# Scores in 64x64 quarters of the array, block sums of the values in column strips, and the weights' low parts on GpSimd, in an attention + ReLU² feed-forward kernel

## The chip, the cores and the metric

The kernel runs on one core of a Trainium2 chip. The metric is the device time of one execution in microseconds (us), smaller is better. The core has a matrix engine (PE in the profile), a vector engine (DVE), an activation engine (ACT), a general one (POOL, called GpSimd in the code) and a queue that issues the transfers (SP). Three runs of the kernel before gave a median of 666.93 us (666.03 to 668.0).

## The reference

What is computed, cut to its core (4 batches, 8 heads, 768 tokens, head size 64, in 32-bit floats):

```python
k_sum = k.reshape(B, H, nb, 32, D).max(axis=3)        # nb = 24 blocks of 32 keys
v_sum = v.reshape(B, H, nb, 32, D).mean(axis=3)
mask_l = np.abs(pos[:, None] - pos[None, :]) < 16
scores_l = where(mask_l, scale * q @ k.T, -1e9)
scores_s = scale * q @ k_sum.T + np.log(32)
a = softmax(concatenate([scores_l, scores_s]))
x = (a @ concatenate([v, v_sum])).transpose(0, 2, 1, 3).reshape(3072, 512)
h = x @ w_in                                          # 512 -> 2048
out = (np.maximum(h, 0) ** 2) @ w_out                 # 2048 -> 512
```

## The kernel before, in words

**Attention.** The 3072 tokens are cut into 48 groups `g` of 64 queries, twelve to a batch. Each group sees 118 keys: the 24 block maxima, and the 94 keys that its window can reach. The steps of one group, with the names of its tasks:

- `S` (L462): scores. Four matmuls, one for each pair of heads, 128 rows x 118 columns. The host lays the queries of a pair out as a 128x128 block with zeros off the diagonal, so that the two heads of a pair don't mix (`qW`, 256 KB a group).
- `M`, `X` (DVE, L484 and L494), `E` (ACT, L503), `R` (DVE, L512 and L513), `N` (POOL, L519): mask and scale, row maximum, exponentials, reciprocal of the sum, and its product.
- `T`: the weights are transposed so that keys lie on partitions. For `g < NPE` (16) on PE (L532) with a copy by ACT; for the others on DVE in 32x32 squares (L549), which then go out to DRAM (L560) and back (L566) to bring the squares to their places.
- `V` (L578): values. Eight matmuls, one for each head, 118 rows x 64 columns; even heads land in the upper and odd heads in the lower 64 columns of the array.
- `XH` (ACT, L588), `XL` (DVE, L591): the result is split into a high part, rounded to the matrix engine's one-pass 32-bit form, and a low part.

**Feed-forward.** A unit `u` is 8 groups (512 tokens), and there are six; 16 hidden blocks `f` of 128 make up 96 items. An item is 12 matmuls of the input product (`FI`, L676, tile `h`: high x high, low x high, high x low for four slices of 128), ReLU and square, a split again, and 12 matmuls of the output product (`FO`, L702, tile `o`). In the last item of a unit `FO` is cut into four pieces, one for each tile of 128 tokens, and each is copied out (`PC`, L727 and L729).

**Weights and values.** The weights arrive as 64-bit floats and are turned into high and low parts in the first unit (`WM` ACT, `WR` `WJ` `WS` DVE L624 L630 L636, `WH` ACT L641, low part `WW` DVE L644), 32 times. The block means of the values: `batch_v_pe` for batches 0 and 1 (six matmuls 24x512 against a matrix of 1/32, `VM` L355, and one copy); `batch_v` for batches 2 and 3 (sums on DVE, L389, and small transfers, L413, from a second layout of `v`).

**What sets the order.** `Plan` simulates the engines with a cost for each task, a due time and the buffers' slots, and writes the instructions of every engine in that order; at run time each engine works its list off in order, held by semaphores. PSUM (the matrix engine's output memory) holds eight banks: four `o`, two `h`, two `att`. `att` serves in turn the scores, the transposes, the values and the block sums of batch 1; before unit 0 the scores use the four `o` banks.

Of the kernel before, what the change touches and what calls it, by code (L numbers as in the profile page):

```python
# [10 lines left out]
F32 = mybir.dt.float32  # L11
# [9 lines left out]
P = 128  # L21
BLOCK = 32
WINDOW = 16
TQ = 64
# [9 lines left out]
NPE = 16  # L34
# [139 lines left out]
def attention_then_relu2_ffn(  # L174
# [4 lines left out]
    v: bass.AP,  # L179
# [5 lines left out]
    B, H, S, D = v.shape  # L185
# [27 lines left out]
    def o_buf(name, cols=512):  # L213
        return buf("o", 4, (P, cols), F32, name, ps)
# [4 lines left out]
    def att_buf(name, cols=512):  # L219
        return buf("att", 2, (P, cols), F32, name, ps)  # L220
# [10 lines left out]
    T0, SLOW, STEP = 35.0, 7.1, 6.5  # L231
# [55 lines left out]
    for g in reversed(range(NG)):  # L287
        pairs = (P, NPAIR, P)
        if g < EARLY:
            q_bufs[g], v_bufs[g] = lend(f"qv{g}", pairs, None)  # L290
            p_bufs[g], a_bufs[g] = lend(f"pa{g}", pairs, None)
        else:
            q_bufs[g] = buf("q", 2, pairs, F32, f"q{g}")
# [44 lines left out]
    def batch_v_pe(b):  # L338

        key = wanted(b * NW) - 28 if b else -60  # L340
        out_ps = (att_buf if b else o_buf)(f"vps{b}")
        vs = vs_bufs[b] = buf("vs", 1, (NB, DM), F32, f"vs{b}")
        last = None
        for i in range(S // P):
            x = buf("half", 4, (P, DM), F32, f"fv{b}_{i}") if b else first_v[i]
            whole = b > 0 or i % 2 == 0
            t = add(
                f"FV{b}_{i}", "SP", 0.45,
                lambda i=i, x=x: nc.sync.dma_start(out=x.tile, in_=vS[b, i * P : (i + 1) * P, :]),
                key - 4 + i, behind=None if whole else t, take=[x] if whole else [], use=[] if whole else [x],  # L350
                size=4 * P * DM, begin=key - 10 if b else 0,
            )

            def mm(i=i, x=x):
                nc.tensor.matmul(  # L355
                    out_ps.tile[:NB], lhsT=means[:, i * NB : (i + 1) * NB], rhs=x.tile,
                    start=(i == 0), stop=(i == S // P - 1),
                )

            last = add(  # L360
                f"VM{b}_{i}", "PE", 0.87, mm, key + i, [t, t_means, last],
                take=[out_ps] if i == 0 else [], use=[x] + [out_ps] * (i > 0),
            )
        t_VS[b] = [add(
            f"VS{b}", "ACT", 0.55, lambda: nc.scalar.copy(out=vs.tile, in_=out_ps.tile[:NB]), key + 7, [last],
            take=[vs], use=[out_ps],
        )]

    def batch_v(b):
        key = wanted(b * NW) - 28  # L370
        n = 512 // D
        nq = BLOCK // n
        vs = vs_bufs[b] = buf("vs", 1, (NB, DM), F32, f"vs{b}")
        after = []
        for hg in range(H // 4):
            part = buf("part", 1, (4 * NB, nq + 1, D), F32, f"part{b}_{hg}")
            src = v[b, 4 * hg : 4 * hg + 4].rearrange("h (j r) d -> (h j) r d", r=BLOCK)
            sums = []
            for i in range(nq):
                raw = buf("half", 4, (P, DM), F32, f"vr{b}_{hg}_{i}")  # L380

                def view(raw=raw):
                    return raw.tile[: 4 * NB].rearrange("p (r d) -> p r d", d=D)

                def load(i=i, src=src, view=view):
                    nc.sync.dma_start(out=view(), in_=src[:, i * n : (i + 1) * n, :])

                def reduce(i=i, part=part, view=view):
                    nc.vector.tensor_reduce(  # L389
                        out=part.tile[:, i, :], in_=view().rearrange("p r d -> p d r"), op=ALU.add, axis=AX.X  # L390
                    )

                t = add(f"VL{b}_{hg}_{i}", "SP", 0.45, load, key, take=[raw], size=4 * 96 * 512, begin=key - 4)
                sums.append(
                    add(f"VR{b}_{hg}_{i}", "DVE", 1.02, reduce, key + 1, [t],
                        take=[part] if i == 0 else [], use=[raw] + [part] * (i > 0))
                )
                if i:
                    sums[-1].after.append(sums[0])

            def total(part=part):
                x = part.tile
                nc.vector.tensor_reduce(
                    out=x[:, nq, :], in_=x[:, :nq, :].rearrange("p i d -> p d i"), op=ALU.add, axis=AX.X
                )
                nc.vector.tensor_scalar_mul(x[:, nq, :], x[:, nq, :], 1.0 / BLOCK)

            t = add(f"VT{b}_{hg}", "DVE", 0.75, total, key + 2, sums, use=[part])
            for hh in range(4):

                def put(hh=hh, hg=hg, part=part):
                    h = 4 * hg + hh
                    nc.sync.dma_start(out=vs.tile[:, h * D : (h + 1) * D], in_=part.tile[hh * NB : (hh + 1) * NB, nq, :])  # L413

                first = hg == hh == 0
                after.append(
                    add(f"VP{b}_{hg}_{hh}", "SP", 0.45, put, key + 3, [t] + after[:1],
                        take=[vs] if first else [], use=[part] + [vs] * (not first), size=6144)
                )
        t_VS[b] = after  # L420


    def attention(g):
# [7 lines left out]
        lq = add(f"QL{g}", "SP", 0.45, lambda: nc.sync.dma_start(out=q.tile, in_=qW[g]), due - 26, take=[q], size=4 * P * DM, begin=due - 36)  # L431
# [26 lines left out]
        s_ps = (o_buf if g < UG else att_buf)(f"s{g}", NPAIR * KEYS)  # L458

        def scores():  # L460
            for p in range(NPAIR):
                nc.tensor.matmul(  # L462
                    s_ps.tile[:, p * KEYS : (p + 1) * KEYS], lhsT=q.tile[:, p, :], rhs=kb[:, p, k0 : k0 + KEYS],
                    start=True, stop=True,
                )
# [3 lines left out]
        t_S[g] = add(f"S{g}", "PE", 0.95, scores, due - 15, deps, take=[s_ps], use=[q])  # L469
# [11 lines left out]
        def masked():  # L481
            if pr.first:
                nc.gpsimd.memset(pr.tile[:, :, KEYS:], 0.0)  # L483
            nc.vector.scalar_tensor_tensor(  # L484
                out=pr.tile[:, :, :KEYS], in0=s_ps.tile.rearrange("p (n k) -> p n k", k=KEYS),
                scalar=1.0 / math.sqrt(D), in1=masks[off].unsqueeze(1).broadcast_to([P, NPAIR, KEYS]),
                op0=ALU.mult, op1=ALU.add,
            )
# [38 lines left out]
        if wide:  # L527
            at_ps = att_buf(f"t{g}")
# [43 lines left out]
        x_ps = (h_buf if g < UG else att_buf)(f"x{g}", NPAIR * TQ)  # L572
        old = [t_FI[(g - RING) // UG, NF - 1]] if g >= RING else []

        def values():
            av = a.tile.rearrange("k (i n r) -> k i n r", i=NSQ, n=NPAIR)
            for h in range(H):
                nc.tensor.matmul(  # L578
                    x_ps.tile[h % 2 * D : (h % 2 + 1) * D, h // 2 * TQ : (h // 2 + 1) * TQ],
                    lhsT=vv.tile[:KEYS, h * D : (h + 1) * D],  # L580
                    rhs=av[:KEYS, h % 2 * 2 : h % 2 * 2 + 2, h // 2, :], start=True, stop=True,
                )
# [4 lines left out]
        def high():  # L587
            nc.scalar.copy(out=xh[:, :, cols], in_=x_ps.tile.rearrange("p (n t) -> p n t", n=NPAIR))  # L588

        def low():  # L590
            nc.vector.tensor_tensor(  # L591
                out=xl[:, :, cols], in0=x_ps.tile.rearrange("p (n t) -> p n t", n=NPAIR),
# [10 lines left out]
    def convert(f, n):  # L603
# [39 lines left out]
        def low():  # L643
            nc.vector.tensor_tensor(  # L644
# [10 lines left out]
        t7 = add(f"WW{name}", "DVE", 0.7, low, due - 4.5, [t6], use=[w, t])  # L655
# [5 lines left out]
    def ffn(u, f, o, done):  # L661
# [37 lines left out]

        def outer(todo):  # L700
            for t, i in todo:
                nc.tensor.matmul(  # L702
                    o[t].tile, lhsT=terms[i][0].tile[:, t * P : (t + 1) * P], rhs=terms[i][1].tile,
# [9 lines left out]
        for i, piece in enumerate(pieces):  # L713
# [3 lines left out]
                take=[o[i]] if first else [], use=[gh, gl] + ([] if first else [o[i]] if last else o),  # L717
            )
            done.append(t6)
            if last:  # L720
                put(u, i, o[i], t6, due + 0.1 * i)

    def put(u, i, o, t, due):
        rows = slice(u * TU + i * P, u * TU + (i + 1) * P)
        x = buf("half", 4, (P, DM), F32, f"os{u}_{i}")
        if i % 2:
            t2 = add(f"PC{u}_{i}", "ACT", 0.62, lambda: nc.scalar.copy(out=x.tile, in_=o.tile), due + 0.6, [t], take=[x], use=[o])  # L727
        else:
            t2 = add(f"PC{u}_{i}", "DVE", 0.7, lambda: nc.vector.tensor_copy(out=x.tile, in_=o.tile), due + 0.6, [t], take=[x], use=[o])  # L729
# [4 lines left out]
    batch_v_pe(0)  # L734
    done_g = 0

    def groups(n):
        nonlocal done_g
        while done_g < n:
            g = done_g  # L740
            b, w = divmod(g, NW)
            if b and not w:
                batch_k(b)
                (batch_v_pe if b < 2 else batch_v)(b)
# [8 lines left out]
    for u in range(NU):  # L753
        groups((u + 1) * UG)
        o = [o_buf(f"o{u}_{t}") for t in range(NTT)]
# [56 lines left out]
```

## Time and profile before

| what | before |
|---|---|
| median of three runs | 666.93 us (666.03 to 668.0) |
| profiled execution | 667.02 us |
| its span (first to last instruction) | 665.3 us |
| PE busy | 643.5 us, 97% |
| DVE / ACT / POOL busy | 340.3 / 278.6 / 83.6 us |
| mean granted clock of PE | 0.994 |

The span lies 1.7 us under the profiled execution's time; that execution stands within 0.1 us of the median. A matrix product of two full 32-bit operands (scores, values, block sums) is two instructions on PE, and one of the one-pass form (`FI`, `FO`) is one; so `x8` behind a score row is a group's four matmuls.

### The profile page before, as it was taken

Reading aid. Unit: us, or ns where it says so; the run is one execution under the profiler, and the core shown is the slowest. Engines: PE = TensorE matmul, PEld = TensorE weight load, DVE = VectorE, ACT = ScalarE, POOL = GpSimd, SP = SyncE. Lnnn points to the kernel's source line nnn. Section 1 sums busy time; section 2 is a strip of 40 time slices with the busy share of each in tenths; the row PEclk is TensorE's granted clock in tenths of the full one; section 3 lists DMA queues with packets and bytes.
Section 4 is the critical chain, followed back from the end, with each engine's and each line's share of the span. In section 5 each row is a group of like instructions: output and inputs, shape, how many; then the busy total and the mean of one; then the engine's idle time right before and its main releaser. Section 6 shows DMA issues by size and latency. Waiting matters only on the chain.

```text
span 665.3 us, 9719 instructions
## 1 busy us (share of the span) xinstructions
PE 643.5 (97%) x3544; PEld 511.2 (77%) x3544; DVE 340.3 (51%) x612; ACT 278.6 (42%) x751; POOL 83.6 (13%) x140
## 2 busy tenths in 40 slices
PE   4979999999999999999999999899999999999997
PEld 3557668878887878787888877778878888888886
DVE  4698879985433375644434586443553342322222
ACT  2688559775534443433323432233343242222221
POOL 3741001100201001101110200110110010000000
PEclk9979999999999999999999999999999999999999
DMA  9955657502523381633141482322352311000001
GB/s 308 323 196 180 237 213 245 187 24 75 157 76 80 78 256 42 182 88 76 49 115 45 150 254 75 101 73 75 97 149 56 91 34 33 32 33 1 0 1 63
DMA packets 50215, 75.61 MB, mean 114 GB/s; under 512 B 6440, under 2 KB 22824, under 8 KB 50168
## 3 DMA queue, kind: packets, MB, share of 16 engines
q1 hardware_dynamic: 50168, 75.00, 36.8%
q8 instruction: 28, 0.46, 0.3%
q14 instruction: 19, 0.16, 0.1%
HBM read 59.75 MB, written 14.68 MB: 112 GB/s over the span
## 4 chain that ended last, share of the span: by engine, by line
PE 86%; DVE 4%; SPq 4%; DMA 3%; issue 1%; POOL 1%; ACT 0%; DVEq 0%; ACTq 0%; POOLq 0%
PE h L676 38%; PE o L702 37%; PE s L462 6%; PE x L578 4%; PE vps L355 2%; SPq L560 1%; DMA vr<-v 1%; DVE part L389 1%; DMA fv_lent<-vS 1%; PE t L532 1%; SPq L440 1%; SPq L413 1%; POOL qv_lent L443 0%; DMA a<-turn 0%; DMA out<-os 0%
## 5 line engine op out<-in xcount | busy, mean ns | idle before, releaser
L676 PE MATMUL h<-xh,w 128*128 128x512 f32 x768 | 245.7, 401 | 0.5 <-ACT xh L588 0.5
L702 PE MATMUL o<-w,gh 128*128 128x512 f32 x768 | 203.9, 400 | 0.0
L676 PEld LDWEIGHTS h<-xh,w 128*128 128x128 f32 x768 | 143.2, 189 | 35.0 <-issue 0.8
L702 PEld LDWEIGHTS o<-w,gh 128*128 128x128 f32 x768 | 139.8, 188 | 32.3 <-issue 1.7
L676 PE MATMUL h<-xl,w 128*128 128x512 f32 x384 | 152.8, 398 | 0.3 <-DVE xl L591 0.3
L684 ACT ACTIVATE r<-h 128x512 f32<-128x512 f32 x96 | 57.2, 595 | 183.6 <-PE h L676 159.9
L695 DVE TENSOR_TENSOR gl<-r,gh 128x512 fp32r<-128x512 f32 x96 | 69.1, 720 | 85.4 <-PE o L702 53.8
L702 PE MATMUL o<-w,gl 128*128 128x512 f32 x384 | 109.2, 391 | 0.0
L690 DVE TENSOR_TENSOR r<-r 128x512 f32<-128x512 f32 x64 | 44.8, 700 | 96.8 <-ACT r L684 95.7
L692 ACT CAST gh<-r 128x512 fp32r<-128x512 f32 x96 | 59.6, 621 | 77.7 <-PE o L702 48.9
L676 PEld LDWEIGHTS h<-xl,w 128*128 128x128 f32 x384 | 72.7, 189 | 18.5 <-DVE xl L591 1.0
L702 PEld LDWEIGHTS o<-w,gl 128*128 128x128 f32 x384 | 72.1, 188 | 15.8
L503 ACT ACTIVATE p<-p,nm 128x118 f32<-128x118 f32 x160 | 61.1, 384 | 49.0 <-DVE nm L494 49.0
L519 POOL TENSOR_TENSOR p<-p,nm 128x472 f32<-128x472 f32 x40 | 45.1, 1128 | 184.4 <-DVE nm L513 106.9
L474 POOL COPY kb<-kb 128x96 f32<-128x96 f32 x44 | 17.1, 389 | 275.8 <-PE s L462 271.7
L462 PEld LDWEIGHTS s<-kb,q 128*128 128x128 f32 x320 | 41.6, 191 | 5.2 <-POOL p L483 1.2
L462 PE MATMUL s<-kb,q 128*128 128x118 f32 x320 | 42.1, 274 | 1.0 <-POOL p L483 1.0
L484 DVE SCALAR_TENSOR_TENSOR p<-s,mask 128x472 f32<-128x472 f32 x40 | 25.8, 645 | 26.0 <-PE s L462 25.5
L578 PEld LDWEIGHTS x<-a,v 118*64 118x64 f32 x640 | 22.0, 137 | 17.6 <-issue 12.4
L549 DVE STREAM_TRANSPOSE a<-p 128x512 f32<-128x512 f32 x32 | 22.7, 708 | 19.6 <-POOL p L519 19.6
L512 DVE TENSOR_SCALAR nm<-nm 128x4 f32<-128x4 f32 x48 | 8.9, 185 | 44.9 <-ACT p L503 43.5
L578 PE MATMUL x<-a,v 118*64 118x64 f32 x640 | 27.4, 228 | 3.5 <-DMA a<-turn 2.9
(55 smaller groups left out, 423.3 us busy)
## 6 DMA issues: line engine op xcount, KB each, us to landing
raw<-wW SPq DMA_DIRECT2D x32, 512.0 KB
q<-qW SPq DMA_DIRECT2D x40, 256.0 KB
turn<-a SPq DMA_DIRECT2D x128, 64.0 KB
a<-turn SPq DMA_DIRECT2D x32, 256.0 KB
v<-vS SPq DMA_DIRECT2D x36, 192.0 KB
kb<-kT SPq DMA_DIRECT2D x16, 384.0 KB
out<-os SPq DMA_DIRECT2D x24, 256.0 KB
vr<-v SPq DMA_DIRECT2D x16, 192.0 KB
```

Source lines behind the costliest of these rows:

```text
L462: nc.tensor.matmul(s_ps.tile[:, p * KEYS : (p + 1) * KEYS], lhsT=q.tile[:, p, :], rhs=kb[:, p, k0 : k0 + KEYS], start=True, stop=True,)
L484: nc.vector.scalar_tensor_tensor(out=pr.tile[:, :, :KEYS], in0=s_ps.tile.rearrange("p (n k) -> p n k", k=KEYS), scalar=1.0 / math.sqrt(D), ...
L503: nc.scalar.activation(x, x, AF.Exp, bias=nm.tile[:, p : p + 1], scale=1.0, accum_out=nm.tile[:, NPAIR + p : NPAIR + p + 1],)
L519: nc.gpsimd.tensor_tensor(out=x, in0=x, in1=nm.tile[:, 2 * NPAIR :].unsqueeze(2).broadcast_to([P, NPAIR, KEYS]), op=ALU.mult)
L549: nc.vector.transpose(out=a.tile.rearrange("p (j n r) -> p j n r", j=NSQ, n=NPAIR), in_=pr.tile.rearrange("p n (j c) -> p j n c", c=SQ),)
L578: nc.tensor.matmul(x_ps.tile[h % 2 * D : (h % 2 + 1) * D, h // 2 * TQ : (h // 2 + 1) * TQ], lhsT=vv.tile[:KEYS, h * D : (h + 1) * D], rhs= ...
L676: nc.tensor.matmul(h.tile, lhsT=lhs.tile[:, k * P : (k + 1) * P], rhs=rhs[:, k, c0 : c0 + TU], start=(i == 0), stop=(i == 3 * KT - 1),)
L684: t2 = add(f"RL{u}_{f}", "ACT", 0.62, lambda: nc.scalar.activation(r.tile, h.tile, AF.Relu), due + 3, [t1], take=[r], use=[h])
L690: lambda: nc.vector.tensor_tensor(out=r.tile, in0=r.tile, in1=r.tile, op=ALU.mult), due + 4, [t2], use=[r],
L692: t4 = add(f"GH{u}_{f}", "ACT", 0.62, lambda: nc.scalar.copy(out=gh.tile, in_=r.tile), due + 5, [t3], take=[gh], use=[r])
L695: lambda: nc.vector.tensor_tensor(out=gl.tile, in0=r.tile, in1=gh.tile.bitcast(F32), op=ALU.subtract),
L702: nc.tensor.matmul(o[t].tile, lhsT=terms[i][0].tile[:, t * P : (t + 1) * P], rhs=terms[i][1].tile, start=(first and i == 0), stop=(last an ...
```

## The change

Five things change.

1. **Scores.** Each head is a matmul of its own, 64 rows x 64 columns of the array: `score_of(h)` gives the quarter and the place. Heads of a pair `p` read rows 0-63 (even) and 64-127 (odd); the columns alternate, so that the four heads of two pairs name all four quarters. The host stores the queries without the zeros, 128 KB a group.
2. **PSUM.** One tile `att` of two banks is no longer two slots: scores take its columns 0-117 in four slices, the values take columns 192-255 or 128-191 (two slots). The scores thus have one slot. The four `o` tiles become two, each of two banks, and a tile of 128 tokens is a half of one. Transposes and block sums take `h` slots.
3. **Transposes.** `NPE` is 8: groups 8 to 15 are transposed by DVE and sent through DRAM, as those from 16 on were.
4. **Block sums.** All four batches take the matrix engine; each 24x512 matmul is cut into four of 24x128, each in its own strip of 32 columns, and four copies gather them. The sums on DVE and the second layout of `v` are gone.
5. **Low parts of the weights** (`WW`) go from DVE to POOL. The planner's constants change with it (`T0`, `STEP`, the costs of `S`, `VM`, `VS`, `WW`).

```diff
-NPE = 16
+NPE = 8
...
+    att = ps.tile([P, 4, 256], F32, name="att", bufs=1)
+            kinds["s"] = Slots(None, "s", 1, [att])
+            kinds["x"] = Slots(None, "x", 2, [att[:, :, 256 - (i + 1) * TQ : 256 - i * TQ] for i in range(2)])
+    def score_of(h):
+        p, r = divmod(h, 2)
+        return 2 * r + p // 2, r ^ p % 2
...
-                nc.tensor.matmul(
-                    out_ps.tile[:NB], lhsT=means[:, i * NB : (i + 1) * NB], rhs=x.tile,
-                    start=(i == 0), stop=(i == S // P - 1),
-                )
+                for c in range(NSQ):
+                    nc.tensor.matmul(
+                        out_ps.tile[c * SQ : c * SQ + NB, :P], lhsT=means[:, i * NB : (i + 1) * NB],
+                        rhs=x.tile[:, c * P : (c + 1) * P], start=(i == 0), stop=(i == S // P - 1),
+                    )
...
-            for p in range(NPAIR):
+            for h in range(H):
+                p, r = divmod(h, 2)
+                j, c = score_of(h)
+                rows = slice(r * D, (r + 1) * D)
                 nc.tensor.matmul(
-                    s_ps.tile[:, p * KEYS : (p + 1) * KEYS], lhsT=q.tile[:, p, :], rhs=kb[:, p, k0 : k0 + KEYS],
-                    start=True, stop=True,
+                    s_ps.tile[c * TQ : (c + 1) * TQ, j, :KEYS],
+                    lhsT=q.tile[rows, p, :], rhs=kb[rows, p, k0 : k0 + KEYS], start=True, stop=True,
                 )
...
-            nc.vector.tensor_tensor(
+            nc.gpsimd.tensor_tensor(
                 out=w.tile[:, DM:], in0=t.tile, in1=w.tile[:, :DM].bitcast(F32), op=ALU.subtract
             )
...
+        def o_of(o, t):
+            return o[t // 2].tile.rearrange("p (a b) c -> p a (b c)", a=2)[:, t % 2]
...
-                take=[o[i]] if first else [], use=[gh, gl] + ([] if first else [o[i]] if last else o),
+                take=[o[i // 2]] if first and i % 2 == 0 else [],
+                use=[gh, gl] + ([o[i // 2]] * (i % 2) if first else [o[i // 2]] if last else o),
```

Where instructions move is seen on PE at three places.

First, the start of the program on PE before: scores (`s`), block sums of batch 0 (`vps`), transposes (`t`) and values (`x`).

```order
L462 MATMUL s_167<-kb,qv_lent 128x118 x4
L462 MATMUL s_180<-kb,qv_lent 128x118 x4
L355 MATMUL vps_190<-fv_lent,means 24x512
L462 MATMUL s_203<-kb,qv_lent 128x118 x4
L355 MATMUL vps_190<-fv_lent,means 24x512 x2
L532 MATMUL t_230<-ident,pa_lent 128x128 x4
L355 MATMUL vps_190<-fv_lent,means 24x512
L462 MATMUL s_241<-kb,qv_lent 128x118 x4
L355 MATMUL vps_190<-fv_lent,means 24x512
L532 MATMUL t_254<-ident,pa_lent 128x128 x4
```

And the same place on PE after the change, up to the first values (`att`).

```order
L434 MATMUL s_166<-kb,qv_lent 64x118 x8
L375 MATMUL vps_182<-fv_lent,means 24x128 x4
L434 MATMUL s_189<-kb,qv_lent 64x118 x8
L375 MATMUL vps_182<-fv_lent,means 24x128 x8
L434 MATMUL s_220<-kb,qv_lent 64x118 x8
L375 MATMUL vps_182<-fv_lent,means 24x128 x12
L434 MATMUL s_262<-kb,qv_lent 64x118 x8
L504 MATMUL t_279<-ident,pa_lent 128x128 x4
L504 MATMUL t_294<-ident,pa_lent 128x128 x4
L434 MATMUL s_304<-kb,qv_lent 64x118 x8
L551 MATMUL att<-pa_lent,qv_lent 64x64 x8
```

Three scores stand ahead of the first transpose before and four after, all block sums of batch 0 are done ahead of the first transpose, and the numbers of matmuls double for scores and go fourfold for block sums. On DVE, the list ahead of the last low part (`XL`) of unit 0's values holds four `WJ`, three `WS`, two `WW` and nine `M` before, and two `WJ`, two `WS`, no `WW` and ten `M` after; its other work there is the same.

Second, the end of unit 1 on PE, where batch 2 begins. Before, the scores of a group (`s`) stand between the input product of the unit's last item (`h`) and an output product (`o`); no block sums stand there.

```order
L676 MATMUL h_15_2451<-xl,w_15_1565 128x512
L462 MATMUL s_2468<-kb,q_2271 128x118 x4
L702 MATMUL o_0_1805<-w_13_1547,gh_13_2389 128x512 x2
L702 MATMUL o_1_1838<-w_13_1547,gh_13_2389 128x512 x2
L702 MATMUL o_2_1850<-w_13_1547,gh_13_2389 128x512 x2
L702 MATMUL o_3_1867<-w_13_1547,gh_13_2389 128x512 x2
L702 MATMUL o_0_1805<-w_13_1547,gl_13_2414 128x512
```

After the change the six pieces of batch 2's block sums (`vps`) lie between the products of the unit's last items.

```order
L375 MATMUL vps_2493<-fv_1_2463,means 24x128 x4
L678 MATMUL o_0_1902<-w_12_1546,gh_12_2425 128x512 x4
L678 MATMUL o_1_1947<-w_12_1546,gh_12_2425 128x512 x4
L678 MATMUL o_0_1902<-w_12_1546,gl_12_2437 128x512 x2
L678 MATMUL o_1_1947<-w_12_1546,gl_12_2437 128x512 x2
L375 MATMUL vps_2493<-fv_2_2465,means 24x128 x4
L551 MATMUL att<-a_2427,v_74 64x64 x8
L375 MATMUL vps_2493<-fv_3_2468,means 24x128 x4
L434 MATMUL att<-kb,q_2482 64x118 x8
L375 MATMUL vps_2493<-fv_4_2511,means 24x128 x4
```

Each of these pieces waits for one load of 128 tokens of `v`; scores, values and block sums now stand side by side between two products.

Third, the last output products on PE, with the semaphores that they wait for. Before, the four tiles `o_0` to `o_3` follow each other, and only the first waits for its operands.

```order
L702 MATMUL o_0_5181<-w_15_1610,gl_15_5567 128x512 [waits DVE_49]
L702 MATMUL o_1_5199<-w_15_1610,gh_15_5565 128x512 x2
L702 MATMUL o_1_5199<-w_15_1610,gl_15_5567 128x512
L702 MATMUL o_2_5203<-w_15_1610,gh_15_5565 128x512 x2
L702 MATMUL o_2_5203<-w_15_1610,gl_15_5567 128x512
L702 MATMUL o_3_5207<-w_15_1610,gh_15_5565 128x512 x2
L702 MATMUL o_3_5207<-w_15_1610,gl_15_5567 128x512
```

After, each of the two tiles holds two outputs, and the second output of a tile waits for the copy of the first.

```order
L678 MATMUL o_0_5332<-w_15_1703,gl_15_5716 128x512 [waits DVE_49]
L678 MATMUL o_0_5332<-w_15_1703,gh_15_5714 128x512 [waits DVE_49]
L678 MATMUL o_0_5332<-w_15_1703,gh_15_5714 128x512
L678 MATMUL o_0_5332<-w_15_1703,gl_15_5716 128x512
L678 MATMUL o_1_5353<-w_15_1703,gh_15_5714 128x512 x2
L678 MATMUL o_1_5353<-w_15_1703,gl_15_5716 128x512
L678 MATMUL o_1_5353<-w_15_1703,gh_15_5714 128x512 [waits DVE_49]
L678 MATMUL o_1_5353<-w_15_1703,gh_15_5714 128x512
```

The two waits for DVE in the rows `o_0 ... gh` and `o_1 ... gh` are new; they are for the copies of the first and the third output (L705 of the new kernel).

More of the change, by code (lines that the diff above doesn't have):

```diff
@@ L360, in batch_v_pe @@
             last = add(
-                f"VM{b}_{i}", "PE", 0.87, mm, key + i, [t, t_means, last],
+                f"VM{b}_{i}", "PE", 0.3, mm, key + i, [t, t_means, last],
                 take=[out_ps] if i == 0 else [], use=[x] + [out_ps] * (i > 0),
             )
[L364 to L420, printed above, removed]
@@ L423, in attention, with gather @@
+        def gather():
+            for c in range(NSQ):
+                nc.scalar.copy(out=vs.tile[:, c * P : (c + 1) * P], in_=out_ps.tile[c * SQ : c * SQ + NB, :P])
+        t_VS[b] = [add(f"VS{b}", "ACT", 1.1, gather, key + 7, [last], take=[vs], use=[out_ps])]
     def attention(g):
@@ L429, in attention @@
         wide = NPE > g
-        lq = add(f"QL{g}", "SP", 0.45, lambda: nc.sync.dma_start(out=q.tile, in_=qW[g]), due - 26, take=[q], size=4 * P * DM, begin=due - 36)
+        lq = add(f"QL{g}", "SP", 0.45, lambda: nc.sync.dma_start(out=q.tile, in_=qW[g]), due - 26, take=[q], size=2 * P * DM, begin=due - 36)
         def load_v():
@@ L484, in masked @@
             nc.vector.scalar_tensor_tensor(
[L485 removed]
+                out=pr.tile[:, :, :KEYS], in0=s_ps.tile[:, :, :KEYS],
                 scalar=1.0 / math.sqrt(D), in1=masks[off].unsqueeze(1).broadcast_to([P, NPAIR, KEYS]),
@@ L587, in high @@
         def high():
-            nc.scalar.copy(out=xh[:, :, cols], in_=x_ps.tile.rearrange("p (n t) -> p n t", n=NPAIR))
+            nc.scalar.copy(out=xh[:, :, cols], in_=x_ps.tile)
         def low():
             nc.vector.tensor_tensor(
-                out=xl[:, :, cols], in0=x_ps.tile.rearrange("p (n t) -> p n t", n=NPAIR),
+                out=xl[:, :, cols], in0=x_ps.tile,
                 in1=xh[:, :, cols].bitcast(F32), op=ALU.subtract,
@@ L654, in convert @@
         t6 = add(f"WH{name}", "ACT", 0.62, high, due - 5.5, [t5], take=[w], use=[t])
-        t7 = add(f"WW{name}", "DVE", 0.7, low, due - 4.5, [t6], use=[w, t])
+        t7 = add(f"WW{name}", "POOL", 1.25, low, due - 4.5, [t6], use=[w, t])
         t_W[n, f] = [t6, t7]
@@ L726, in put @@
         if i % 2:
-            t2 = add(f"PC{u}_{i}", "ACT", 0.62, lambda: nc.scalar.copy(out=x.tile, in_=o.tile), due + 0.6, [t], take=[x], use=[o])
+            t2 = add(f"PC{u}_{i}", "ACT", 0.62, lambda: nc.scalar.copy(out=x.tile, in_=o_tile()), due + 0.6, [t], take=[x], use=[o])
         else:
-            t2 = add(f"PC{u}_{i}", "DVE", 0.7, lambda: nc.vector.tensor_copy(out=x.tile, in_=o.tile), due + 0.6, [t], take=[x], use=[o])
+            t2 = add(f"PC{u}_{i}", "DVE", 0.7, lambda: nc.vector.tensor_copy(out=x.tile, in_=o_tile()), due + 0.6, [t], take=[x], use=[o])
         add(f"PS{u}_{i}", "SP", 0.45, lambda: nc.sync.dma_start(out=out[rows, :], in_=x.tile), due + 1, [t2], use=[x], size=4 * P * DM)
     batch_k(0)
-    batch_v_pe(0)
+    batch_v(0)
     done_g = 0
@@ L754, in attention_then_relu2_ffn @@
         groups((u + 1) * UG)
-        o = [o_buf(f"o{u}_{t}") for t in range(NTT)]
+        o = [o_buf(f"o{u}_{t}") for t in range(NTT // 2)]
         for f in range(NF):
```

53 lines of the change are left out of this document (28 added, 25 removed).

## The prediction, as made before the changed kernel was run

> **What bounds the kernel now.** I read the page first, for the busy shares and the chain that ended last.
>
> ```profile
> span 665.3 us, 9719 instructions
> PE 643.5 (97%) x3544; PEld 511.2 (77%) x3544; DVE 340.3 (51%) x612; ACT 278.6 (42%) x751; POOL 83.6 (13%) x140
> PE 86%; DVE 4%; SPq 4%; DMA 3%; issue 1%; POOL 1%; ACT 0%; DVEq 0%; ACTq 0%; POOLq 0%
> PE h L676 38%; PE o L702 37%; PE s L462 6%; PE x L578 4%; PE vps L355 2%; SPq L560 1%; DMA vr<-v 1%; DVE part L389 1%; DMA fv_lent<-vS 1%; PE t L532 1%; SPq L440 1%; SPq L413 1%; POOL qv_lent L443 0%; DMA a<-turn 0%; DMA out<-os 0%
> ```
>
> PE is the bound: it carries 86% of the chain, and three quarters of the chain are feed-forward products, which the change leaves alone. What is to be had lies in scores (6%), values, block sums and transposes, and where PE waits. The windows by stage show where it waits (columns: window, us, then busy us and instructions of PE, PEld, DVE, ACT, POOL, the granted clock, DMA share, GB/s).
>
> ```profile
> 10.00:20.00 10.00, 9.43 (x31) 4.55 (x30) 4.85 (x13) 5.12 (x25) 2.91 (x8) 1.00 1.05 339
> 20.00:30.00 10.00, 8.48 (x78) 6.01 (x78) 6.33 (x15) 7.41 (x31) 6.27 (x14) 1.00 1.05 317
> 30.00:40.00 10.00, 7.74 (x106) 6.59 (x104) 9.74 (x20) 8.04 (x27) 8.37 (x15) 1.00 0.63 222
> 100.00:120.00 20.00, 20.00 (x126) 16.45 (x125) 18.36 (x36) 18.03 (x46) 3.22 (x4) 1.00 0.74 250
> 400.00:500.00 100.00, 97.09 (x553) 78.53 (x552) 48.31 (x87) 34.37 (x104) 12.54 (x16) 1.00 0.35 96
> ```
>
> From 100 us on PE is full; before, DVE is (9.74 of 10 us from 30 to 40). So there are two regimes: in the steady part every piece on PE costs its own length; at the start the end is set by when the first input product can begin.
>
> **Scores.** The chain of waits from 215 us gives pieces as start, length and what; each length runs to the next start.
>
> ```profile
> 218.07 2.80 PE h L676 x12
> 220.87 0.88 PE s L462 x8
> 221.75 2.76 PE o L702 x12
> 224.51 0.61 PE x L578 x16
> 225.13 3.00 PE h L676 x12
> 228.13 2.76 PE o L702 x12
> ```
>
> A group's scores cost 0.88 us: eight instructions of 118 columns, 0.11 each, one after another. The values show what half-width pieces do: 16 instructions take 0.61, and the product behind them 3.00 instead of 2.80, so 0.81 in all. If one 64-column pass takes 0.11 x 64/118 = 0.06, sixteen in a row would take 0.96; two halves side by side take 0.48. A timeline cut at three ends shows how they start (the columns are start, length, what, and the count inside the window).
>
> ```profile
> 314.97 0.28 PE L578 MATMUL x<-a,v 118*64 118x64 f32 x2
> 314.97 0.39 PE L578 MATMUL x<-a,v 118*64 118x64 f32 x6
> 311.24 0.26 PE L462 MATMUL s<-kb,q 128*128 128x118 f32 x1
> ```
>
> The first window ends at 315.00, the second at 315.14: two have started after 0.03 us, six after 0.17, so a pair starts every 0.06. The third is the same cut for the scores of before: 0.08 us in, one has started. So halves do run side by side, and values pay 0.81 - 0.48 = 0.33 us for going into that mode and out of it. I take the same for quarters: sixteen passes of 118 columns, four at a time, 4 x 0.11 = 0.44, plus 0.33, is **0.77 us** against 0.88. No row shows four quarters, so the price is bounded: without the 0.33 it is 0.44 (-16.7 us in all); with two at a time 0.88 + 0.33 = 1.21 (+12.5); with none 1.76 + 0.33 = 2.09 (+46). I take 0.77 since the nearest row, the values, shows both concurrency and the 0.33. Of the 48 groups 38 stand behind the first input product: 38 x 0.11 = **-4.2 us**.
>
> [...]
>
> **Transposes and block sums.** Pieces from the same view at 70 and 82 us.
>
> ```profile
> 70.56 0.44 PE t L532 x4
> 82.55 0.97 PE vps L355 x2
> 83.52 2.95 PE o L702 x12
> ```
>
> Eight groups' transposes leave PE: 8 x 0.44 = **-3.5**. They put 8 x 0.71 us on DVE (the price of L549), and a trip through DRAM; the new order has three to four items of feed-forward (2.80 + 2.76 us each) between their scores and values, 17 us and more, which covers it. Without that cover the wait would be one like those in the next fence, 1.8 us each.
>
> A block sum costs 0.97 and 2.95 - 2.76 = 0.19 behind it, 1.16. Its two passes take 0.485 each for 512 columns, so 0.12 for 128. Four strips at once are 2 x 0.12 + 0.33 = 0.57; two at once 0.82. For batch 1 that is 6 x (0.57 - 1.16) = **-3.5** (two at once: -2.0; no mode cost: -5.5). Batches 2 and 3 put twelve such pieces on PE that were not there: 6.8, and as some stand side by side with values, **+6.5** (+2.9 to +9.8). In return the sums leave DVE, and with them the waits there.
>
> ```profile
> PE x L578 <- DMA a<-turn: 2.9, 2, 1.8
> PE x L578 <- DMA out<-os: 0.6, 1, 0.6
> 254.47 2.94 DVE part L389 x3
> 263.84 1.96 SPq L560
> ```
>
> The first two rows are waits of PE (total, times, longest); the next two are pieces of the chain at 254 us, where three sums on DVE push the softmax of a group back, and the queue of SP is long with small transfers. With sums and transfers gone I take both waits as gone: **-3.5** (0 to -3.5). What is late next there is the block sums' load: it takes staging buffers (`half`) that the outputs of the unit before also use; nothing in PE's list behind it is short of work, so a late load costs its piece's wait once.
>
> **The start.** Chain of waits and timeline from 11 to 46 us.
>
> ```profile
> 11.48 2.06 PE s L462 x8
> 13.54 1.83 PE vps L355 x2
> 16.71 1.83 PE vps L355 x4
> 20.10 1.08 PE s L462 x8
> 30.15 0.65 DVE pa_lent L484
> 39.73 1.70 DVE t L630 x2
> 41.43 0.60 DVE t L636
> 44.02 1.01 DVE w L644
> 44.51 1.22 PE L676 MATMUL h<-xh,w 128*128 128x512 f32 x2 [0.47 <-ACT xh L588]
> ```
>
> The first input product starts at 44.51. Up to 24.8 us the chain is PE, with scores and block sums in turn; from 30 us on it is DVE without a gap. Ahead of the last low part DVE loses two `WJ` (1.70), one `WS` (0.60) and two `WW` (0.71 each, next fence), and gets one `M` more (0.65): 3.1 us less. On PE the six block sums shrink (1.83 for two instructions at that clock) and half the query bytes go, but scores, masks and values now hold one another through the one `att` tile. I take half of 3 us there: together **-4.5** (0, if the transfers set the pace; -8, if PE's and DVE's savings both come through).
>
> **The low parts on POOL.**
>
> ```profile
> L519 POOL TENSOR_TENSOR p<-p,nm 128x472 f32<-128x472 f32 x40 | 45.1, 1128 | 184.4 <-DVE nm L513 106.9
> L644 DVE TENSOR_TENSOR w<-t,w 128x512 fp32r<-128x512 f32 x32 | 22.5, 707 | 2.9 <-ACT w L641 2.9
> ```
>
> A product of 472 columns takes POOL 1.128 us, so 512 take an estimated 1.22 against 0.707 on DVE. 32 x 1.22 = 39 us spread over unit 0, where POOL is busy 3.2 of 20 us and DVE 18.4 (row from 100 us): it costs nothing as long as POOL has nothing ahead of it; behind a normalisation it comes 1.1 us late.
>
> **The end.** Timeline of the last products.
>
> ```profile
> 659.38 0.62 PE L702 MATMUL o<-w,gh 128*128 128x512 f32 x2
> 659.58 0.69 DVE L729 COPY os<-o 128x512 f32<-128x512 f32 x1 [5.42 <-PE o L702]
> 660.06 0.62 PE L702 MATMUL o<-w,gh 128*128 128x512 f32 x2
> ```
>
> Before, the second output starts at 659.38 while the first is copied (659.58 to 660.27). With two outputs in one tile it waits for the copy's end: 0.9 us, twice, **+1.8**.
>
> **Small waits.** The same at five earlier unit ends, where other work can stand in; values that wait for the mask of the scores just ahead (same banks); products that wait for low parts on POOL. Nothing to 38 x 0.1 + 5 x 0.9 = 8.3; I take **+2.5**, near the low end, since at most places an item of 5.6 us lies between.
>
> **Sum**, against the profiled execution's 667.0 (0.1 above the median, 1.7 above its span): -4.2 - 3.5 - 3.5 + 6.5 - 3.5 - 4.5 + 1.8 + 2.5 = -8.4, so **658.6 us**.
>
> **Rivals.**
> *A, slower: only two quarters overlap.* Both passes of a head stand next to each other and need the same quarter; if an instruction can't start before the one ahead has started, the second pass blocks the next head's first. Then only two of the four are ever at work: scores cost 1.21 instead of 0.77 (+16.7), eighteen block sums 0.25 more each (+4.5): **680**. It decides from 0.99 us a group on (0.77 + 8.4/38). Against it: the values' first two started within 0.03 us though the second pass of the same head stands between them by program order. For it: that is two tiles, not four, and no row shows row halves. Chance 0.14. [...]
> *B: the start gives nothing and POOL is late.* +4.5, and sixteen items of unit 0 wait half of the 0.5 us by which a low part is longer, +4: **667.1**. For it: the DMA share reads 1.05 from 10 to 30 us. Chance 0.15.
> *C: more than forecast.* The mode cost is half for quarters (-6.3) and the start gives -7: **650**. Chance 0.10.
> *D: the quarters don't overlap at all*, scores 2.09: **709** and above with block sums. The values' rows speak against it. Chance 0.03.
> The forecast has 0.58, with 654 to 663 for its own bounds.
>
> **How the numbers follow.** Forecast, B and C hold 0.83 together, and lie between 650 and 668: that is the range. A measurement tells 0.3% (2 us) from no change, so same is 665 to 669: most of B, 0.11. Faster: the forecast, C and 0.02 of B, 0.70. Slower: A, D and 0.02 of B, 0.19.
>
> **What would show it.** In the chain of the changed kernel a scores piece with what it adds to the piece behind it: 0.77 if right, 1.21 for A. A block sum at 0.57. No transposes on PE behind the first input product but those of early groups; that product at 40 us. No wait for `a<-turn` over 1 us at the starts of batches 2 and 3; two gaps of 0.9 in the last 4 us. The forecast is wrong if scores cost over 0.99, if the first product starts later than 44.5, or if values of groups 8 to 15 wait for DRAM.

## The result, and the profile after

| | before | after |
|---|---|---|
| median | 666.19 us (12 runs, 664.59 to 668.0) | 669.86 us (12 runs, 668.22 to 671.41) |
| ratio, 95% interval | 1 | 1.0053 (1.0041 to 1.0064) |
| profiled execution | 667.02 us | 668.47 us |
| PE / DVE / POOL busy | 643.5 / 340.3 / 83.6 us | 632.4 / 332.2 / 126.6 us |

The kernel became half a per cent slower, though PE has 11 us less to do. The head of the page and the shares of the chain of waits after the change:

```profile
span 666.8 us, 10794 instructions
PE 632.4 (95%) x4064; PEld 482.9 (72%) x4064; DVE 332.2 (50%) x564; ACT 277.2 (42%) x757; POOL 126.6 (19%) x172
PE 76%; DVE 14%; DMA 3%; issue 2%; ACT 2%; POOL 1%; SPq 1%; DVEq 0%; POOLq 0%
```

DVE's share of the chain rose from 4% to 14%, PE's fell from 86% to 76%. Where that lies is in the windows (columns as in the prediction: window, us, then busy us of PE, PEld, DVE, ACT, POOL, the clock, DMA):

```profile
40.00:60.00 20.00, 17.89 (x89) 12.89 (x89) 18.62 (x26) 14.46 (x33) 11.21 (x10) 0.88 0.46 127
60.00:80.00 20.00, 19.71 (x122) 14.83 (x122) 19.96 (x30) 13.32 (x34) 8.60 (x6) 1.00 0.96 325
80.00:100.00 20.00, 18.06 (x155) 12.96 (x154) 17.32 (x30) 12.63 (x32) 8.55 (x8) 1.00 0.74 241
100.00:120.00 20.00, 17.29 (x97) 12.26 (x96) 19.96 (x27) 12.11 (x30) 10.52 (x8) 1.00 0.61 191
120.00:140.00 20.00, 17.99 (x115) 13.74 (x114) 19.90 (x29) 14.85 (x39) 11.70 (x10) 1.00 0.50 168
140.00:200.00 60.00, 58.30 (x364) 44.57 (x363) 29.06 (x51) 30.78 (x81) 11.80 (x14) 1.00 0.35 99
```

Before, PE was full from 60 to 200 us. Now it is idle for 2.1 + 0.3 + 1.9 + 2.7 + 2.0 + 1.7 = 10.7 us between 40 and 200 us, and DVE is full (19.9 and more of 20) in three of the four windows from 60 to 140 us, in which weights are converted. Unit 0 as a whole, from its first input product to the end of its last output copy, first before, then after:

```profile
44.51:171.08 126.57, 126.28 (x684) 97.24 (x685) 102.67 (x191) 87.61 (x206) 14.05 (x18) 0.98 0.46 162
170.49 0.59 ACT L727 COPY os<-o 128x512 f32<-128x512 f32 x1 [0.52 <-PE o L702]
40.07:171.07 131.00, 120.32 (x760) 88.74 (x761) 115.14 (x169) 84.87 (x205) 59.20 (x50) 0.98 0.58 184
170.48 0.59 ACT L704 COPY os<-o 128x512 f32<-128x512 f32 x1 [1.07 <-PE o L678]
```

Unit 0 starts 4.4 us earlier and gives PE 6.0 us less to do, but PE idles 10.7 us in it instead of 0.3, and the unit ends at 171.1 us as before. What was gained there is lost there. So unit 0 changed its bound from PE to DVE, although the low parts had left DVE. The groups of instructions show why: first before, then after (columns: busy us and mean ns of one; then idle time ahead).

```profile
L630 DVE SCALAR_TENSOR_TENSOR t<-t,raw 128x512 uint32<-128x512 uint32 x32 | 23.2, 729 | 2.8 <-ACT t L621 2.8
L636 DVE SCALAR_TENSOR_TENSOR t<-raw,t 128x512 uint32<-128x512 uint32 x32 | 22.6, 705 | 0.0
L624 DVE TENSOR_SCALAR raw<-raw 128x512 uint32<-128x512 uint32 x32 | 15.0, 483 | 0.0
```

```profile
L668 DVE TENSOR_TENSOR gl<-r,gh 128x512 fp32r<-128x512 f32 x96 | 76.0, 791 | 93.8 <-PE o L678 50.1 <-ACT gh L665 43.0
L603 DVE SCALAR_TENSOR_TENSOR t<-t,raw 128x512 uint32<-128x512 uint32 x32 | 26.2, 832 | 0.1
L609 DVE SCALAR_TENSOR_TENSOR t<-raw,t 128x512 uint32<-128x512 uint32 x32 | 26.2, 830 | 0.1
L597 DVE TENSOR_SCALAR raw<-raw 128x512 uint32<-128x512 uint32 x32 | 23.4, 746 | 1.1 <-DMA raw<-wW 1.1
L617 POOL TENSOR_TENSOR w<-t,w 128x512 fp32r<-128x512 f32 x32 | 46.0, 1441 | 49.0 <-ACT w L614 45.3 <-PE att L434 3.6
```

The same DVE instructions take longer: the shift 746 ns instead of 483, the two bit operations 832 and 830 instead of 729 and 705, the split of the hidden block (`gl`) 791 instead of 720. That is 8.4 + 3.0 + 3.6 + 6.9 = 21.9 us, about as much as the 22.5 us of low parts that left DVE. A timeline at 100 us, DVE and POOL alone, shows one such place:

```profile
100.09 1.61 POOL L617 TENSOR_TENSOR w<-t,w 128x512 fp32r<-128x512 f32 x1 [2.22 <-ACT w L614]
100.48 1.77 DVE L668 TENSOR_TENSOR gl<-r,gh 128x512 fp32r<-128x512 f32 x1
102.18 0.68 DVE L609 SCALAR_TENSOR_TENSOR t<-raw,t 128x512 uint32<-128x512 uint32 x1
```

The split on DVE starts while POOL's product runs, and ends 0.55 us behind it (102.25 against 101.70): it took 1.77 us, and the bit operation behind it, alone again, 0.68. PE in its turn waits for DVE's late results; its largest wait from 35 to 200 us is one for low parts:

```profile
PE h L649 <- POOL w L617: 4.5, 6, 1.3
```

Ahead of four of these six waits POOL itself had stood idle for 1.9 to 2.7 us until ACT had the high part, which stands behind the bit operations of DVE.

The parts that were to gain did gain. Pieces of the chain at 310 us, and block sums at 255 us:

```profile
312.11 0.56 PE att L434 x16
312.68 2.93 PE o L678 x12
...
255.10 0.35 PE vps L375 x8
255.44 2.96 PE o L678 x12
...
258.40 2.78 PE h L649 x12
```

Scores take 0.56 and add 0.17 to 0.2 to the piece behind them, 0.75 in all (before 0.88); a block sum 0.35 + 0.20 = 0.55 (before 1.16). A timeline cut 0.06 us behind the scores' start shows four instructions under way at once:

```profile
312.04 0.33 PE L434 MATMUL att<-kb,q 64*64 64x118 f32 x4
```

The first input product starts 4.4 us earlier than before, at 40.07; and at the end PE waits for the copies, as the bracket says:

```profile
40.07 1.22 PE L649 MATMUL h<-xh,w 128*128 128x512 f32 x2 [1.15 <-ACT xh L561]
...
659.38 0.74 PE L678 MATMUL o<-w,gh 128*128 128x512 f32 x2 [0.78 <-DVE os L706]
661.82 0.74 PE L678 MATMUL o<-w,gh 128*128 128x512 f32 x2 [0.78 <-DVE os L706]
```

### The profile page after: what moved, and what is told of

It is laid out like the page before. It is cut to its first block, busy times and chain, and to the rows that moved or that the text cites. A ratio compares the mean times of both kernels' runs of the same rounds, so it can differ in the third digit from the quotient of the medians.

```text
span 666.8 us, 10794 instructions
## 1 busy us (share of the span) xinstructions
PE 632.4 (95%) x4064; PEld 482.9 (72%) x4064; DVE 332.2 (50%) x564; ACT 277.2 (42%) x757; POOL 126.6 (19%) x172
## 4 chain that ended last, share of the span: by engine, by line
PE 76%; DVE 14%; DMA 3%; issue 2%; ACT 2%; POOL 1%; SPq 1%; DVEq 0%; POOLq 0%
PE o L678 35%; PE h L649 34%; PE att L551 3%; PE att L434 3%; DVE t L603 3%; DVE raw L597 2%; DVE t L609 2%; DVE gl L668 2%; DMA raw<-wW 2%; POOL w L617 1%; DMA fv_lent<-vS 1%; DVE nm L466 1%; DVE a L521 1%; DVE os L706 1%; PE vps L375 1%
## 5 line engine op out<-in xcount | busy, mean ns | idle before, releaser
L668 DVE TENSOR_TENSOR gl<-r,gh 128x512 fp32r<-128x512 f32 x96 | 76.0, 791 | 93.8 <-PE o L678 50.1
L491 POOL TENSOR_TENSOR p<-p,nm 128x472 f32<-128x472 f32 x40 | 40.9, 1024 | 137.4 <-DVE nm L485 111.2
L446 POOL COPY kb<-kb 128x96 f32<-128x96 f32 x44 | 20.1, 457 | 228.6 <-PE att L434 222.7
L617 POOL TENSOR_TENSOR w<-t,w 128x512 fp32r<-128x512 f32 x32 | 46.0, 1441 | 49.0 <-ACT w L614 45.3
L521 DVE STREAM_TRANSPOSE a<-p 128x512 f32<-128x512 f32 x40 | 28.2, 706 | 19.5 <-POOL p L491 18.3
L456 DVE SCALAR_TENSOR_TENSOR p<-att,mask 128x472 f32<-128x472 f32 x40 | 25.7, 642 | 23.0 <-PE att L434 22.4
L551 PEld LDWEIGHTS att<-a,v 118*64 118x64 f32 x640 | 21.9, 137 | 15.6 <-issue 8.1
L614 ACT CAST w<-t 128x512 fp32r<-128x512 f32 x32 | 19.7, 617 | 26.7 <-DVE t L609 26.7
L475 ACT ACTIVATION_READ_ACCUMULATOR p<-p,nm 128x1 f32 x160 | 30.0, 187 | 0.0
```

The costliest lines, as they stand in the source:

```text
L456: nc.vector.scalar_tensor_tensor(out=pr.tile[:, :, :KEYS], in0=s_ps.tile[:, :, :KEYS], scalar=1.0 / math.sqrt(D), in1=masks[off].unsqueeze ...
L475: nc.scalar.activation(x, x, AF.Exp, bias=nm.tile[:, p : p + 1], scale=1.0, accum_out=nm.tile[:, NPAIR + p : NPAIR + p + 1],)
L491: nc.gpsimd.tensor_tensor(out=x, in0=x, in1=nm.tile[:, 2 * NPAIR :].unsqueeze(2).broadcast_to([P, NPAIR, KEYS]), op=ALU.mult)
L521: nc.vector.transpose(out=a.tile.rearrange("p (j n r) -> p j n r", j=NSQ, n=NPAIR), in_=pr.tile.rearrange("p n (j c) -> p j n c", c=SQ),)
L551: nc.tensor.matmul(x_ps.tile[h % 2 * D : (h % 2 + 1) * D, h // 2, :], lhsT=vv.tile[:KEYS, h * D : (h + 1) * D], rhs=av[:KEYS, 2 * c : 2 * ...
L617: nc.gpsimd.tensor_tensor(out=w.tile[:, DM:], in0=t.tile, in1=w.tile[:, :DM].bitcast(F32), op=ALU.subtract)
```

## The experiments

Theory 1: a product on POOL holds DVE up, unit 0 is bound by DVE, and what PE saves there becomes waiting. Rivals: the eight transposes overload DVE and DRAM's transfers (theory 2), or the one tile for scores and values ties the engines together (theory 3). All kernels but one start from the changed one; ratios are to the kernel before.

**Low parts left out.** This kernel leaves out the low parts of the weights (a copy of the weight by ACT stands in their place), so it does not compute the reference's result.

```diff
-            nc.gpsimd.tensor_tensor(
-                out=w.tile[:, DM:], in0=t.tile, in1=w.tile[:, :DM].bitcast(F32), op=ALU.subtract
-            )
+            nc.scalar.copy(out=w.tile[:, DM:], in_=t.tile)
```

> The changed kernel, with the low parts of the weights left out: in their place ACT copies the weight once more (32 copies of about 0.62 us), so that neither POOL nor DVE has that work. Theory 1 (products of POOL on SBUF hold up DVE's operations with two SBUF operands and its shifts, unit 0 is bound by DVE, and PE's savings became waits there): L597 back from 0.75 to under 0.55 us, the split of the hidden block in unit 0 back under 0.72, PE idle from 40 to 150 us under 4 us, time 659 to 662 us. Theory 2 (the eight transposes that DVE and DRAM took over overload unit 0) and theory 3 (the one tile for scores and values ties PE and DVE together): PE stays idle for 8 us there, time 667 or more.

Measured 661.94 us, 0.9924 (0.9902 to 0.9946): 7.9 us less than the changed kernel.

```profile
L609 DVE SCALAR_TENSOR_TENSOR t<-raw,t 128x512 uint32<-128x512 uint32 x32 | 21.4, 682 | 0.1
L603 DVE SCALAR_TENSOR_TENSOR t<-t,raw 128x512 uint32<-128x512 uint32 x32 | 21.4, 683 | 2.0 <-ACT t L594 1.7
L597 DVE TENSOR_SCALAR raw<-raw 128x512 uint32<-128x512 uint32 x32 | 15.2, 478 | 9.6 <-DMA raw<-wW 9.6
```

The shift is back at 478 ns, `gl` at 703; PE's waits from 45 to 200 us come to 3.0 us (from 40 to 150 us PE idles 4.3, a little over the 4 expected). Transposes and the tile were the same, so theories 2 and 3 can't be the main cause. The order of the instructions did change with the edit, since the plan makes it from the costs; the experiment on POOL's load below is free of that.

**Low parts on DVE; transposes on PE; both.** (`gpsimd` to `vector` in the lines above; `NPE = 16`.)

> The changed kernel with the low parts of the weights back on DVE. Theory 1: DVE gets 32 x 0.70 = 22.5 us of work and loses about 24 us of being held up, so it stays nearly full in unit 0, but PE no longer waits for a product on POOL (4.5 us): 663 to 667 us. Theory 2 and theory 3: DVE is as full as before and has 22 us more: 672 or more.

> The changed kernel with the transposes of groups 8 to 15 back on PE. Theory 1: DVE loses 5.7 us of work in unit 0, L597 stays at about 0.75, PE gets 3.5 us more, which fits into its idle time: 665 to 668 us. Theory 2: the cause is gone, 660 to 663 us. Theory 3: 669 to 672 us.

> The changed kernel with both undone: low parts on DVE and transposes of groups 8 to 15 on PE. Theory 1: DVE's load in unit 0 is what it was before the change, PE is the bound again, and scores, block sums and start keep their gain: 660 to 664 us. Theory 3: 667 or more.

Measured 669.46 (1.0040, 1.0018 to 1.0062), 676.86 (1.0152, 1.0133 to 1.0170) and 665.69 (0.9995, 0.9978 to 1.0012). None of the three came within theory 1's numbers, nor within theory 3's. Theory 2 fell: transposes on PE cost 7.0 us where the low parts are on POOL, and save 3.8 where they are on DVE. The waits of PE from 45 to 200 us say what else is there; `a_ww_dve`, then `a_npe16` (total us, times, longest):

```profile
PE vps L375 <- DMA fv<-vS: 4.6, 4, 1.6
PE att L551 <- DMA a<-turn: 2.2, 2, 1.5
PE o L678 <- DVE w L617: 1.3, 2, 1.0
```

```profile
PE att L551 <- issue: 3.4, 1, 3.4
PE t L504 <- POOL p L491: 2.6, 2, 1.7
```

With the low parts back on DVE, PE waits for the loads of batch 1's block sums (`fv`) and for transposes from DRAM. With transposes on PE and low parts on POOL, PE waits for the normalisation (`p`). POOL isn't the late one there: ahead of the two normalisations it stands idle for 1.0 and 3.3 us, and starts 0.14 and 0.15 us behind DVE's reciprocal, so the softmax steps on the full DVE are late. For the longest wait, 3.4 us ahead of values, the profile names no releaser; it ends 0.1 us after DVE has masked the scores ahead (to 138.85), which lie in the same tile, so theory 3 may have a share in it. And the granted clock fell at this wait; windows of `a_npe16`:

```profile
136.00:138.00 2.00, 0.00 (x0) 0.00 (x0) 1.90 (x3) 1.88 (x4) 2.00 (x2) 1.00 0.00 0
138.00:140.00 2.00, 1.04 (x16) 0.96 (x16) 2.00 (x5) 0.51 (x1) 0.02 (x1) 0.53 0.00 0
142.00:144.00 2.00, 2.00 (x6) 1.54 (x5) 1.81 (x6) 1.00 (x2) 0.65 (x1) 0.50 0.18 58
144.00:146.00 2.00, 2.00 (x10) 1.66 (x9) 1.72 (x2) 0.87 (x3) 2.00 (x2) 0.76 0.04 8
```

The granted clock goes from 1.00 to 0.50 near the end of the wait and back some 7 us later (0.53 from 138 to 140 us puts the fall at 138.1, 0.76 from 144 to 146 the return at 145.0). In 2 us at 0.50 PE has 6 instructions (142.3 to 144.3), in 2 us at 1.00 it has 10 (146.3 to 148.3); half of some 6.9 us is another 3.4 us, the author's estimate of what the low clock cost. In `a_ww_dve` the clock fell as well (0.74 from 80 to 100 us), though no single wait of PE there is longer than 1.6 us. In the changed kernel, whose waits in unit 0 are 1.3 us at most, it reads 1.00 from 60 to 200 us, and 0.88 from 40 to 60.

**The low parts' load on POOL, with nobody waiting for it.** On `a_ww_act`:

```diff
...
+            nc.gpsimd.tensor_tensor(out=spare_tile, in0=spare_tile, in1=spare_tile, op=ALU.mult)
...
+        add(f"WD{name}", "POOL", 1.25, spare, due - 4.5, [t6])
```

> The kernel of a_ww_act (weights' low parts left out, a copy by ACT in their place) with 32 products of 128x512 on POOL added that work on a spare tile of their own, which nothing waits for; the order on PE and DVE is the same to the last row. If products of POOL hold DVE up by themselves (theory 1), L597 and the conversions' other steps on DVE are stretched by some 10 to 20 us in all and the time rises by 3 to 7 us over a_ww_act's 661.9: 665 to 669. If the cost of the low parts on POOL is only that their results come late, nothing changes: 660 to 663.

Measured 665.33 us (663.44 to 667.17), 0.9984 (0.9970 to 0.9998), against 661.94 (658.65 to 662.86) without the products. The instructions of PE, DVE and ACT stand in the same order in both traces. DVE's conversions are stretched, though no data links them to the spare tile:

```profile
L604 DVE SCALAR_TENSOR_TENSOR t<-t,raw 128x512 uint32<-128x512 uint32 x32 | 26.2, 833 | 0.5 <-ACT t L595 0.4
L610 DVE SCALAR_TENSOR_TENSOR t<-raw,t 128x512 uint32<-128x512 uint32 x32 | 25.2, 801 | 0.1
L598 DVE TENSOR_SCALAR raw<-raw 128x512 uint32<-128x512 uint32 x32 | 20.7, 650 | 3.7 <-DMA raw<-wW 3.7
L624 POOL TENSOR_TENSOR spare<-spare 128x512 f32<-128x512 f32 x32 | 38.3, 1196 | 1.5
```

833, 801 and 650 ns against 683, 682 and 478 in `a_ww_act`: 14.1 us. So POOL's products hold DVE by themselves, and 3.4 us of the 7.9 come from that alone. The other 4.5 come in the kernel in which products wait for POOL's results (4.5 us of PE's waits) and in which DVE's conversions are held longer, 18.1 us instead of 14.1; these two aren't told apart.

**The same part on the kernel before.**

> The kernel before with one part of the change alone: the low parts of the weights on POOL. Theory 1: DVE gives 22.5 us away and gets about as much back in being held up, and products wait for POOL: PE is no longer full from 60 to 140 us, 668 to 673 us. If low parts on POOL are free there, as the prediction had it: 664 to 667.

Measured 679.66 us, 1.0207 (1.0190 to 1.0224), 13.4 us above the kernel before as measured beside it (666.31) and beyond theory 1's 668 to 673: the part alone costs more than it does inside the change. The first row of PE's waits names what is missing in the changed kernel, transposes on PE that wait for the normalisation. Ahead of these three normalisations, too, POOL stands idle (1.3 to 4.3 us) until DVE's reciprocal is there, so they are late by DVE and not by the low parts in POOL's list. In the changed kernel DVE has these transposes.

```profile
PE t L532 <- POOL p L519: 8.4, 3, 5.0
PE h L676 <- POOL w L644: 2.2, 2, 1.2
```

**The order at the end.** On the changed kernel (`a_tail`), and on `a_ww_dve_npe16` (`a_both_tail`):

```diff
-            pieces = [[x for x in todo if x[0] == t] for t in range(NTT)]
+            pieces = [[x for x in todo if x[0] == t] for t in ((0, 2, 1, 3) if last else range(NTT))]
...
```

> The changed kernel with the last output products of each unit in the order of tiles 0, 2, 1, 3 and nothing else: the two gaps at the end of 0.9 us each go, 1.9 us less, and 0.2 to 0.4 at each earlier unit end: 667 to 668 us. If the end is set by copies and transfers: 669.9.

> The kernel of a_ww_dve_npe16 with the last output products of each unit in the order of tiles 0, 2, 1, 3, so that a copy runs beside a product of the other tile: 1.4 to 2.2 us less than its 665.7 us, 663.5 to 664.3; the gaps of 0.9 us at the end go. If the end is set by the copies and transfers out anyway: 665.7.

Measured 667.18 (1.0011, 0.9998 to 1.0024), 2.7 us less than the changed kernel; and 662.28 (0.9949, 0.9934 to 0.9964), 3.4 less than without it and more than the 1.4 to 2.2 expected.

**The loads of batch 1's block sums.** More staging buffers (`half` 6 for 4), or the sums six microseconds later in PE's list:

> The kernel of a_both_tail with six staging buffers in place of four, so that the loads for batch 1's block sums need not wait for a weight's conversion to free one. If those loads cost the 4.7 us of PE's wait and 2 us of low clock behind it in a_ww_dve_npe16: 657 to 660 us, and no wait of vps for fv over 0.5 us. If the transfers are limited by their rate and not by the buffers: 663 to 665.

> The kernel of a_both_tail with the block sums of batch 1 six microseconds later in PE's list and their loads as early as they were. If the products of a_both_tail stand behind block sums whose loads are late (5.4 us of waits, and about 2 us of low clock behind them), both shrink: waits of vps for fv under 2 us, 656 to 660 us. If the loads only follow (staging buffers that weights' conversions hold), the waits stay and the time too: 662.

Measured 661.87 (0.9947, 0.9927 to 0.9966) and 664.40 (0.9964, 0.9943 to 0.9984): no gain by either. Later sums still waited 4.8 us for `fv` (5.4 in `a_both_tail`), so their loads follow: they need staging buffers that conversions on DVE set free. With six buffers the waits went, and another took their place:

```profile
PE h L649 <- ACT vs L387: 3.1, 1, 3.1
PE h L649 <- ACT xh L561: 1.0, 1, 1.0
PE vps L375 <- DMA fv<-vS: 0.5, 2, 0.3
```

Block sums hold one of the two `h` tiles until ACT has gathered them, and the next input product waits for that.

**Block sums of batches 2 and 3 on DVE again**, then with five buffers and the gathering copies first on ACT:

```diff
-                batch_v(b)
+                (batch_v_pe if b < 2 else batch_v)(b)
...
```

> The kernel of a_both_tail with the block sums of batches 2 and 3 on DVE again, as before the change. By the prediction's terms twelve pieces of 0.57 leave PE (-6.5) and two waits for transposes come back (+3.5): 3 us less, 659.3, all of it behind 240 us. If those waits came from something else, or don't come back: 655.5 to 657. If they cost more than the pieces: over 662.

> The kernel of a_both_tail_v23 with five staging buffers and the gathering copies of the block sums ahead of other work on ACT. In a_both_tail_half6 two more buffers took the waits for fv from 5.4 to 0.5 us, but the next product then waited 3.1 us for ACT's gathering copies, since block sums hold one of its two tiles. If both are the cost of batch 1's block sums: 654 to 658 us, waits of vps for fv and of h for vs under 2 us together. If one of the two always takes the other's place: 659 to 662.

Measured 660.08 us, 0.9900 (0.9873 to 0.9926), 2.2 less than `a_both_tail`, with 3.3 us of waits for `a<-turn` back; and 658.55 us, 0.9875 (0.9843 to 0.9906), the fastest here, 8.1 us under the kernel before as measured beside it (666.61). There the waits for `fv` and for `vs` come to 1.5 and 0.8 us. The intervals of the last two overlap, so what the five buffers add isn't settled.

## Why the prediction was wrong

- **Scores** (0.77 for 0.88): right, 0.75. Four instructions run at once; rivals A and D fell. The 0.33 for going into a mode and out of it was the author's estimate from the values. The runs show 0.75 - 0.44 = 0.31 us beyond the estimated four passes, of which 0.17 to 0.2 lie in the product behind the scores; what causes it they don't show.
- **Block sums** (0.57, with the same 0.33 in it): right, 0.55, of which 0.20 lie in the product behind. In batches 2 and 3 the waits went as forecast, and the twelve new pieces cost more than they: 2.2 us by the medians of `a_both_tail` and `a_both_tail_v23`, 3.0 by the terms.
- **The start** (-4.5): right for the first product, 44.51 to 40.07, but unit 0 ended no earlier (171.1 us). Two instructions of a block sum took 1.83 us at 13.54 and 0.97 later (82.55); that the clock made the difference is not shown, the windows read 1.00 at both places.
- **The end** (+1.8): the two waits are near the forecast (0.78 each); with the earlier unit ends, `a_tail` gives 2.7.
- **The low parts on POOL**: the step that failed. "It costs nothing as long as POOL has nothing ahead of it" priced POOL and DVE apart. In the trace DVE got back 21.9 of the 22.5 us by being held, POOL's product took 1.44 instead of the estimated 1.22, and PE stood still for 10.7 us in unit 0, where all small waits of the kernel together had been put at 2.5. By the terms unit 0 was to end some 12 us earlier, and it ended when it did before; behind it the terms add up to some +4, and the span grew by 1.5. So unit 0 holds the whole of the 9.9 us by which the profiled execution (668.5) missed 658.6. Of the 11.3 us by which the median missed it the low parts account for 7.9 (`a_ww_act`); the other three or so remain with them gone. Rival B's price (667.1) came near, its reason only in part: the first product did start earlier, and POOL was late mostly because DVE was.
- **Transposes** (-3.5) and **batch 1's block sums** (-3.5): PE's work fell, but in a stretch where DVE sets the pace that is worth nothing. The prediction's own row had DVE at 18.36 of 20 us from 100 us on, and the transposes put 5.7 us more on it. With the low parts on DVE (`a_ww_dve`) the transposes' trip cost 3.8 us instead of gaining 3.5: PE waited twice for `a<-turn` (2.2 us), so the cover of three items did not hold there. Where DVE has neither the low parts nor POOL's hold (`a_ww_act`), PE has no such wait from 45 to 200 us.
- **The loads of batch 1's block sums** are a second step that failed: they were put at nothing. With low parts and transposes both undone (`a_ww_dve_npe16`) the terms that are left give some 662 us, and 665.69 were measured; PE waited 4.7 us for `fv` in unit 0, and the clock was 0.83 from 80 to 100 us.

That POOL holds DVE is shown by `a_ww_act_spare`, in which PE, DVE and ACT work off the same lists as in `a_ww_act` and DVE's conversions take 14.1 us more. That DVE's pace is what turns it into PE's waits is read from the windows and from `a_ww_act`; the split into 3.4 and 4.5 us comes from medians of kernels that spread by 2 us and more.

## What to carry to other kernels

Before moving work from DVE to POOL, count it on both: here 46.0 us of low parts on POOL stood against 21.9 us that DVE lost, in operations of the kinds that were held (the first four rows of the table below). A saving on PE is worth its time only where PE is the bound in that stretch, so a change's terms are to be summed stage by stage, each against the engine that is full there. And behind one wait of 3.4 us on PE (`a_npe16`) the granted clock stood at 0.50 for some 7 us, an estimated 3.4 us more.

## What the runs showed of the hardware

From the start and end of each DVE instruction of the changed kernel, apart by whether a POOL instruction ran in more than a tenth of its time (mean ns, count):

| DVE instruction | alone | beside POOL |
|---|---|---|
| split of the hidden block, two operands in SBUF | 689 (82) | 1390 (14) |
| shift, one operand in SBUF | 417 (11) | 918 (21) |
| bit operation L603, two operands in SBUF | 676 (17) | 1009 (15) |
| bit operation L609, two operands in SBUF | 676 (20) | 1086 (12) |
| square of ReLU, two operands in SBUF | 690 (44) | 831 (20) |
| mask and scale, one operand in PSUM | 635 (9) | 644 (31) |
| low part of the values, one operand in PSUM | 414 (26) | 410 (22) |
| row maximum | 642 (35) | 628 (5) |
| transposition in squares | 707 (37) | 697 (3) |

At 100.48 us it was not a sharing of rate: the split lost 1.08 us (1.77 against 0.69) to an overlap of 1.22. Held were the operations with two operands in SBUF (the split by 701 ns, the bit operations by 333 and 410, the square by 141) and the shift (by 501), which has one. The operations with one operand in PSUM, the row maximum and the transposition differ by 14 ns at most. Why the ones are held and the others not is not shown by a run here.
